# A local attention feeding a channel-mix block on one Trainium2 core: the first unit of tokens multiplied in fp32 on weights that are not yet split

## The chip, the cores and the metric

The kernel runs on one core of a Trainium2 chip. TensorE (PE in the profile, with PEld for its weight loads) multiplies into PSUM; VectorE (DVE), ScalarE (ACT) and GpSimd (POOL) work on tiles of 128 partitions; SyncE (SP) issues every DMA. The metric is device time in microseconds of one launch. Three runs of the kernel before gave 420.61, 421.57 and 421.47 us, a median of 421.47 us.

## The reference

Two stages follow one another. The first is attention over short windows: q, k and v are 4 batches x 8 heads x 768 tokens x 64. Tokens stand in chunks of 32, and each chunk sees 8 memory keys, its own 32 keys, 16 to the left and 8 to the right. The second stage is a channel mix over the 512 features that the heads give together:

```python
scores = scale * np.matmul(q_c, k_full.transpose(0, 1, 3, 2))   # per chunk of 32 queries, 64 keys
a = np.exp(scores - max); a = a / (np.sum(a) + 1e-09); out = np.matmul(a, v_full)
...
xk = mu_k * x + (1.0 - mu_k) * x_prev        # x_prev: the token before
xr = mu_r * x + (1.0 - mu_r) * x_prev
k = np.maximum(xk @ w_k, 0.0)                # w_k 512 x 1024
v = k * k @ w_v                              # w_v 1024 x 512
r = 1.0 / (1.0 + np.exp(-(xr @ w_r)))        # w_r 512 x 512
return r * v
```

Here x has 3072 rows (4 x 768) of 512 features. All of it is fp32.

## The kernel before, in words

**Units.** The 3072 tokens are cut into 12 units of 256 tokens (`UTOK`); a unit is two tiles of 128. For each unit the kernel makes scores (PE `s`), a softmax (DVE `mx`, `e`, `sum`; ACT exp on `e`), a transposition of the probabilities (PE `pt`), copies into a block layout (`aTz`), the product with v (PE `px`), a copy to the transposed features `xT`, and then the channel mix: the gate `g` (PE `pr`, two blocks, sigmoid `sg`), the key side `h` (PE `ph`, four blocks, relu and square `kf`) and the value side `v` (PE `pv`, four half blocks), a product with the gate (`o`) and a store.

**Split products.** A product of fp32 accuracy is made of three passes in a reduced format, fp32r: an operand is split into a high part (a cast) and a low part (operand minus high part), and TensorE adds high x high, high x low and low x high. So every weight tile, every `xf` and every `kf` gets a cast and a subtraction (`wkh`/`wkl`, `wvh`/`wvl`, `wrh`/`wrl`, `xh`/`xl`, `kh`/`kl`) ahead of its first product. One block of `g`, `h` or `v` is 12 matmuls of 512 columns or 24 of 256.

**Weights.** The weights come as 64-bit words, ten DMAs of 1 MB into `raw`: two of w_r, four of w_k, four of w_v, in this order. Each needs an ACT pass (`mag`, L270), a DVE shift (L273), a DVE join to fp32 (L277), then the cast and the subtraction (L283).

**Order.** The order on every engine is written ahead of time by a planner in the file. `te_order` gives each PE operation a due time from a list: `LEAD` for the start and one pattern per unit. `Plan.order` then lists operations greedily with an assumed cost for each, and picks an engine where an operation has alternatives; buffer tags with fixed counts (`bufs`) add waits. Where the plan leaves PE idle before the first `ph`, products of zeros or of a weight tile (`warm`, L660 and L663) are put in; L660 holds three lists written out by hand for the three longest gaps.

**Around the change.** `weight` prepares one weight tile, `scores` a unit's softmax, `prep` the two mixes `xf` and their split, `channel_mix` the blocks of `g`, `h` and `v`. The first unit is handled as every other is.

Of the kernel before, what the change touches and what calls it, by code (L numbers as in the profile page):

```python
# [29 lines left out]
LOOK = 400  # L30
EASE = 0.0
LEAD = "s0 t0 t1 a0 a1 s1 g0.0 g0.1"
# [7 lines left out]
BLOCK = 2.65  # L40
PE_COST = {"s": 1.6, "t": 0.4, "a": 1.05, "g": BLOCK, "h": BLOCK, "v": BLOCK}
# [33 lines left out]
class Plan:  # L75
# [40 lines left out]
    def order(self):  # L116
        self.dues()
# [3 lines left out]
        for q in todo.values():  # L121
            q.sort(key=lambda o: (o.due, o.seq))
        done = []
        while len(done) < len(self.ops):
            best = None
            for q in todo.values():
# [20 lines left out]
def te_order():  # L147

    nu = B * S // UTOK
    seq = LEAD.split()  # L150
    seq = [tuple([x[0]] + [int(n) for n in x[1:].split(".")]) for x in seq]
    for u in range(nu):
# [17 lines left out]
def local_attention__then__channel_mix(  # L170
# [31 lines left out]
    def split_tiles(n, name):  # L202
        return [
            [const.tile([P, 2 * DM], F32R, tag=f"{name}{s}{i}", name=f"{name}{s}{i}") for i in range(n)]
            for s in "hl"
        ]

    wk_hl, wv_hl, wr_hl = split_tiles(KT, "wk"), split_tiles(FT // 2, "wv"), split_tiles(KT // 2, "wr")
# [6 lines left out]
    zero_r = const.tile([P, 2 * DM], F32R, tag="zeror", name="zero_r")  # L215
    nc.vector.memset(zero_sb, 0.0)
    nc.vector.memset(zero_r.bitcast(F32), 0.0)
# [24 lines left out]
    wdone = {}  # L242
# [4 lines left out]
    def weight(i):  # L247
        src, (hi, lo), k = chunks[i]
        h, l = hi[k], lo[k]
# [18 lines left out]
        def f_abs():  # L268
            m = T["mag", i] = sb("x4", [P, 2 * DM], f"mag{i}")
# [5 lines left out]
        def f_join():  # L275
            mi = T["mag", i].bitcast(U32)
            nc.vector.scalar_tensor_tensor(mi, mi, 3, word(0, U32), ALU.logical_shift_left, ALU.bitwise_or)  # L277

        def f_hi(e):
            copy(e, h, T["mag", i])  # L280

        def f_lo(e):
            e.tensor_sub(l, T["mag", i], h.bitcast(F32))  # L283

        raw, mag = Slot("big"), Slot("x4")
        a = op(("dma", 3.0), f_load, new=[raw])
# [4 lines left out]
        ll = op(either(dve=(1.15, True), pool=(2.5, True)), f_lo, [hh], use=[mag])  # L291
        wdone[id(hi), k] = (hh, ll)

    def wdeps(hl, ks):
        return [o for k in ks for o in wdone[id(hl[0]), k]]

    xdone = {}
    prior = {}
# [3 lines left out]
    def scores(u):  # L302


        ts = range(u * QPU, (u + 1) * QPU)

# [5 lines left out]
        def f_s():  # L312
            s = T["s", u] = ps("s", f"s{u}", QPU)
            s5 = s.rearrange("p (h c r k) -> p h c r k", h=2, c=QPU, r=NPAIR)
            nq = NPAIR * NJ * CHUNK
            for c, t in enumerate(ts):
                a = T["qk", t]
                q4 = a[:, :nq].rearrange("p (r j q) -> p r j q", r=NPAIR, j=NJ)
                k4 = a[:, nq:].rearrange("p (r j k) -> p r j k", r=NPAIR, j=NJ)
                for r in range(NPAIR):  # L320
                    for j in range(NJ):
                        for h in range(2):
                            z = slice(64 * h, 64 * h + 64)
                            nc.tensor.matmul(  # L324
                                s5[CHUNK * j : CHUNK * (j + 1), h, c, r, :], q4[z, r, j, :], k4[z, r, j, :],
                                start=True, stop=True,
                            )

        def f_max():
            s5 = T["s", u].rearrange("p (h c r k) -> p h c r k", h=2, c=QPU, r=NPAIR)  # L330
            for c, t in enumerate(ts):
                if qts[t][1] == 0:
                    nc.vector.memset(s5[0:CHUNK, :, c, :, 0:LEFT], NEG)
                if qts[t][1] == NQT - 1:
                    nc.vector.memset(s5[P - CHUNK : P, :, c, :, LEFT + CHUNK : LEFT + CHUNK + RIGHT], NEG)
            mx = T["mx", u] = sb("sm", [P, NG], f"mx{u}")
            nc.vector.reduce_max(mx, T["s", u].rearrange("p (g k) -> p g k", k=NK), axis=AX.X)

        def f_sub():
            e = T["e", u] = sb("e", [P, NG, NK], f"e{u}")  # L340
            nc.vector.tensor_sub(  # L341
                e,
                T["s", u].rearrange("p (g k) -> p g k", k=NK),
                T["mx", u].unsqueeze(2).to_broadcast([P, NG, NK]),
            )

        def f_exp():
            e = T["e", u]
            nc.scalar.activation(e, e, AF.Exp, scale=SCALE)  # L349

        def f_sum():
            sm = T["sum", u] = sb("sm", [P, NG], f"sum{u}")
            nc.vector.reduce_sum(sm, T["e", u], axis=AX.X)
            nc.vector.tensor_scalar_add(sm, sm, 1e-9)
            nc.vector.reciprocal(sm, sm)

        def f_norm(g):
            e = T["e", u]
            g.tensor_mul(e, e, T["sum", u].unsqueeze(2).to_broadcast([P, NG, NK]))

        qs = [Slot("big") for _ in ts]
        s1, m1, m2, e = Slot("s"), Slot("sm"), Slot("sm"), Slot("e")
        ds = due["s", u]
        l = [op(("dma", 2.3), lambda t=t: f_load(t), new=[x]) for t, x in zip(ts, qs)]
        o_s = op(("pe", 1.6), f_s, l + [prior.get("s")], new=[s1], use=qs, due=ds)
        o_m = op(("dve", 1.15), f_max, [o_s], new=[m1], use=[s1], due=ds + 4)
        o_b = op(("dve", 1.15), f_sub, [o_m], new=[e], use=[s1, m1], due=ds + 5.5)
        o_e = op(("act", 1.0), f_exp, [o_b], use=[e])
        o_u = op(("dve", 1.55), f_sum, [o_e], new=[m2], use=[e])
        o_n = op(either(dve=(1.15, True), pool=(2.2, True)), f_norm, [o_u], use=[e, m2])  # L370
        prior.update(s=o_s)
        return o_n, e

    def attention(t, o_n, e):
# [54 lines left out]
        lv = op(("dma", 1.5), f_loadv, new=[vs])  # L429
# [13 lines left out]

    def prep(u):
# [9 lines left out]
        for m in (1, 0):  # L454
            def f_mix(m=m):
                d = T["df", u]
                f = T["xf", u, m] = sb("x4", [P, KT, UTOK], f"xf{u}") if m else d
# [19 lines left out]
            fs, hs, ls = Slot("x4") if m else ds, Slot(f"xh{m}"), Slot(f"xl{m}")  # L477
# [239 lines left out]
```

## Time and profile before

The profiled execution took 420.69 us by its own time and has a span of 418.7 us; the 2.0 us between them lie outside the span.

| what | value |
|---|---|
| median of three runs | 421.47 us (420.61 to 421.57) |
| profiled execution, its own time / span | 420.69 / 418.7 us |
| PE busy, PEld busy | 409.4 us (98%), 375.4 us (90%) |
| DVE busy, ACT busy, POOL busy | 261.7 us (63%), 202.9 us (48%), 15.8 us (4%) |
| DMA moved | 48.95 MB, mean 117 GB/s |
| mean granted TensorE clock | 0.988 |

A busy PE counts the `warm` products too, so 98% says little of the start. The stages have to be read apart: the first 85.67 us, in which the first unit is worked off and the weights are prepared, and what follows, which repeats one pattern per unit. In a row of the timeline or of the chain the first number is the start in us from the span's start, the second the duration; in a row of windows, each engine's busy time with the count of its instructions, then the granted clock (PEclk), the busy share of the DMA engines and GB/s.

### The profile page before, as it was taken

Reading aid. Unit: us, or ns where it says so; the run is one execution under the profiler, and the core shown is the slowest. Engines: PE = TensorE matmul, PEld = TensorE weight load, DVE = VectorE, ACT = ScalarE, POOL = GpSimd, SP = SyncE. Lnnn points to the kernel's source line nnn. Section 1 sums busy time; section 2 is a strip of 40 time slices with the busy share of each in tenths; the row PEclk is TensorE's granted clock in tenths of the full one; section 3 lists DMA queues with packets and bytes.
Section 4 is the critical chain, followed back from the end, with each engine's and each line's share of the span. In section 5 each row is a group of like instructions: output and inputs, shape, how many; then the busy total and the mean of one; then the engine's idle time right before and its main releaser. Section 6 shows DMA issues by size and latency. Waiting matters only on the chain.

```text
span 418.7 us, 10166 instructions
## 1 busy us (share of the span) xinstructions
PE 409.4 (98%) x4601; PEld 375.4 (90%) x4601; DVE 261.7 (63%) x351; ACT 202.9 (48%) x281; POOL 15.8 (4%) x22
## 2 busy tenths in 40 slices
PE   8979999999999999999999999999999999999996
PEld 8878898799899899899898898898898898998995
DVE  2888589948729639639639539539539449447121
ACT  1642878345545445455355355364364364363150
POOL 2000001001001001001001001001001001000000
PEclk9995999999999999999999999999999999999999
DMA  8996186413313314314205206205112012100101
GB/s 315 378 363 254 66 298 216 184 52 113 140 52 126 127 50 141 124 42 163 117 25 177 101 27 193 86 29 207 68 36 95 25 57 73 38 13 2 50 2 50
DMA packets 12906, 48.95 MB, mean 117 GB/s; under 512 B 1472, under 2 KB 1600, under 8 KB 12352
## 3 DMA queue, kind: packets, MB, share of 16 engines
q1 hardware_dynamic: 12864, 48.31, 31.6%
q8 instruction: 36, 0.59, 0.6%
q14 instruction: 6, 0.05, 0.0%
HBM read 42.01 MB, written 6.29 MB: 115 GB/s over the span
## 4 chain that ended last, share of the span: by engine, by line
PE 89%; DVE 5%; ACT 3%; DMA 1%; issue 1%; ACTq 0%; SPq 0%
PE pv L588 29%; PE ph L531 29%; PE pr L492 15%; PE px L403 5%; PE s L324 4%; PE warm L660 3%; PE pt L386 2%; PE warm L663 2%; DMA raw<-in_w_v_dram 1%; ACT mag L270 1%; DVE mag L277 1%; DVE raw L273 1%; DVE wvl L283 1%; ACT e L349 1%; ACT wkh L228 0%
## 5 line engine op out<-in xcount | busy, mean ns | idle before, releaser
L531 PE MATMUL ph<-xh,wkh 128*128 128x256 f32 x384 | 107.6, 280 | 0.0
L531 PE MATMUL ph<-xl,wkh 128*128 128x256 f32 x384 | 105.6, 275 | 0.0
L531 PE MATMUL ph<-xh,wkl 128*128 128x256 f32 x384 | 105.6, 275 | 0.0
L540 ACT ACTIVATE kf<-ph 128x512 f32<-128x512 f32 x48 | 28.7, 598 | 113.9 <-PE ph L531 110.2
L531 PEld LDWEIGHTS ph<-xh,wkh 128*128 128x128 f32 x384 | 73.6, 192 | 1.1
L531 PEld LDWEIGHTS ph<-xl,wkh 128*128 128x128 f32 x384 | 73.7, 192 | 0.3
L588 PE MATMUL pv<-wvh,kh 128*128 128x512 f32 x192 | 73.8, 385 | 0.0
L531 PEld LDWEIGHTS ph<-xh,wkl 128*128 128x128 f32 x384 | 73.7, 192 | 0.0
L588 PE MATMUL pv<-wvh,kl 128*128 128x512 f32 x192 | 72.8, 379 | 0.0
L588 PE MATMUL pv<-wvl,kh 128*128 128x512 f32 x192 | 72.8, 379 | 0.0
L557 DVE TENSOR_TENSOR kl<-kf,kh 128x512 fp32r<-128x512 f32 x38 | 26.3, 691 | 55.8 <-ACT kh L228 55.6
L602 DVE TENSOR_TENSOR o<-pv,sg 128x512 f32<-128x512 f32 x24 | 16.6, 690 | 45.1 <-PE pv L588 45.1
L588 PEld LDWEIGHTS pv<-wvh,kh 128*128 128x128 f32 x192 | 36.3, 189 | 5.5
L588 PEld LDWEIGHTS pv<-wvh,kl 128*128 128x128 f32 x192 | 36.3, 189 | 5.1
L588 PEld LDWEIGHTS pv<-wvl,kh 128*128 128x128 f32 x192 | 36.3, 189 | 4.6
L492 PE MATMUL pr<-wrh,xl 128*128 128x512 f32 x96 | 37.3, 388 | 1.0 <-DVE xl L475 1.0
L492 PE MATMUL pr<-wrh,xh 128*128 128x512 f32 x96 | 37.5, 391 | 0.0
L492 PE MATMUL pr<-wrl,xh 128*128 128x512 f32 x96 | 37.3, 388 | 0.0
L547 ACT ACTIVATE kf<-kf 128x512 f32<-128x512 f32 x48 | 30.3, 631 | 1.2
L228 ACT CAST kh<-kf 128x512 fp32r<-128x512 f32 x48 | 29.8, 622 | 1.5
L349 ACT ACTIVATE e<-e 128x1024 f32<-128x1024 f32 x12 | 12.7, 1057 | 34.7 <-DVE e L341 34.7
L459 DVE SCALAR_TENSOR_TENSOR df<-df,mu_sb,xT 128x256 f32<-128x256 f32 x48 | 29.2, 667 | 0.0
(63 smaller groups left out, 547.8 us busy)
## 6 DMA issues: line engine op xcount, KB each, us to landing
qk<-in_qk_dram SPq DMA_DIRECT2D x24, 768.0 KB, 5.8
vw<-in_vw_dram SPq DMA_DIRECT2D x24, 512.0 KB, 4.5
out_dram<-o SPq DMA_DIRECT2D x24, 256.0 KB, 2.0
raw<-in_w_k_dram SPq DMA_DIRECT2D x4, 1024.0 KB, 6.7
raw<-in_w_v_dram SPq DMA_DIRECT2D x4, 1024.0 KB, 6.8
raw<-in_w_r_dram SPq DMA_DIRECT2D x2, 1024.0 KB, 10.4
id_sb<-in_ident_dram SPq DMA_DIRECT2D x1, 64.0 KB, 6.4
mu_sb<-in_mu_dram SPq DMA_DIRECT2D x1, 4.0 KB, 11.6
```

The lines of the kernel that those rows point to most:

```text
L228: e.copy(dst, src)
L324: nc.tensor.matmul(s5[CHUNK * j : CHUNK * (j + 1), h, c, r, :], q4[z, r, j, :], k4[z, r, j, :], start=True, stop=True,)
L349: nc.scalar.activation(e, e, AF.Exp, scale=SCALE)
L403: nc.tensor.matmul(p3[64 * h : 64 * h + 64, 2 * g : 2 * g + 2, CHUNK * j : CHUNK * j + CHUNK], v[:, g, h, j, :], a[:, h, g, j, :], start=True,
L459: nc.vector.scalar_tensor_tensor(f[:, k], d[:, k], mu_sb[:, m, k : k + 1], T["xT", u][:, k, :UTOK], ALU.mult, ALU.add)
L492: nc.tensor.matmul(pairs(p), x[:, k, c * P : (c + 1) * P], woven(w), start=(k + n == 0), stop=(k == KT - 1 and n == 2),)
L531: nc.tensor.matmul(pairs(p[:, i * UTOK : (i + 1) * UTOK]), w[:, fc], x[:, :, k].rearrange("p t n -> p n t"), start=(k + n == 0), stop=(k = ...
L540: e.activation(r, T["ph", u, f], AF.Relu)
L547: e.activation(q, q, AF.Square)
L557: e.tensor_sub(l, T["kf", u, f], T["kh", u, f].bitcast(F32))
L588: nc.tensor.matmul(pairs(p), x[:, tc_], woven(w), start=(f + n == 0), stop=(f == FT - 1 and n == 2))
L602: nc.vector.tensor_mul(o, T["pv", u, c], T["sg", u][:, c * DM : (c + 1) * DM])
```

## The change

The first unit (u = 0) is multiplied whole: `WHOLE = "hgv"` makes its key side, gate and value side plain fp32 products of the unsplit operands with the unsplit weight tiles. For that unit `xf` and `kf` are not split. `prep_first` makes `xf` by 128x256 slices, one ACT scale and one DVE multiply-add each, with 1 - mu from a small POOL operation. The key side of the first unit runs by rows of w_k (`f_row`): one w_k tile at a time adds to all four accumulators, so that a product can begin when the first tile is joined. The first unit's softmax runs tile by tile (`part`, half the columns each), and the second tile's exp and normalization stand ahead of the first weight's ACT pass and join.

The weights are loaded in the order w_k, w_r, w_v. Joined tiles have buffers of their own (`w0` to `w9`), and the low part of tile i goes into the buffer of tile i-1. `later` ties every cast and subtraction of a weight to the end of the first row block. `LEAD` lists the whole first unit, `STRICT` keeps PE in that list for the first 60 operations placed, the hand-written `warm` lists and their zero tile are gone, and `big` has 5 buffers, `sm` 4 and `x4` 3 (before: 4, 2 and 4).

From the key side of unit 1 on, PE's 1883 rows are the same as before in shape and order.

TensorE, from the second `px` of the first unit on, before (`s1` scores of unit 1, `pr0_0` the first gate block):

```order
L403 MATMUL px1_286<-aTz1_87,vw1_105 64x2x32 x16
L663 MATMUL warm_107<-zero_sb_88 128x128
L324 MATMUL s1_310<-qk2_207 32x64 x32
L324 MATMUL s1_310<-qk3_253 32x64 x32
L660 MATMUL warm_107<-wrh0_82 128x256 x10
L660 MATMUL warm_107<-wrh0_82 128x128 x48
L492 MATMUL pr0_0_465<-wrh0_82,xh0_1_392 128x512
L492 MATMUL pr0_0_465<-wrl0_84,xh0_1_392 128x512
L492 MATMUL pr0_0_465<-wrh0_82,xl0_1_402 128x512
```

The same place in the change (`w0` is the first joined w_k tile, `xf0_0` the unsplit key input):

```order
L443 MATMUL px1_270<-aTz1_77,vw1_188 64x2x32 x16
L776 MATMUL warm_90<-zero_sb_78 128x128 x8
L354 MATMUL s1_0_306<-qk2_244 32x64 x32
L354 MATMUL s1_0_306<-qk3_259 32x64 x32
L618 MATMUL ph0_0_382<-xf0_0_291,w0_215 128x256 x2
L618 MATMUL ph0_1_385<-xf0_0_291,w0_215 128x256 x2
L618 MATMUL ph0_2_388<-xf0_0_291,w0_215 128x256 x2
L618 MATMUL ph0_3_391<-xf0_0_291,w0_215 128x256 x2
L618 MATMUL ph0_0_382<-xf0_0_291,w1_263 128x256 x2
```

The key side has moved ahead of the gate, takes its operands unsplit, and no `warm` stands behind the scores of unit 1.

SyncE's queue, the sixth to the twelfth DMA, before:

```order
L256 DMA raw0_189<-in_w_r_dram 128x2x512
L256 DMA raw1_196<-in_w_r_dram 128x2x512
L245 DMA mu_sb_65<-in_mu_dram 128x8
L310 DMA qk2_207<-in_qk_dram 128x1536
L310 DMA qk3_253<-in_qk_dram 128x1536
L254 DMA raw2_284<-in_w_k_dram 128x1024
L254 DMA raw3_376<-in_w_k_dram 128x1024
```

And now, from the fifth on:

```order
L252 DMA raw0_140<-in_w_k_dram 128x1024
L420 DMA vw1_188<-in_vw_dram 128x1024
L243 DMA mu_sb_65<-in_mu_dram 128x8
L252 DMA raw1_195<-in_w_k_dram 128x1024
L330 DMA qk2_244<-in_qk_dram 128x1536
L330 DMA qk3_259<-in_qk_dram 128x1536
L252 DMA raw2_288<-in_w_k_dram 128x1024
```

Two w_k tiles have moved ahead of the scores' operands of unit 1; w_r has moved behind w_k.

VectorE, where the weights' low parts of w_r are made in the change (they stood ahead of the first gate before); `wl3` is the low part of the last w_k tile, `wl4` and `wl5` those of w_r:

```order
L275 SCALAR_TENSOR_TENSOR w9_527<-w9_527,raw9_501 128x1024
L519 TENSOR_TENSOR df1_582<-xT1_565 128x1024
L282 TENSOR_TENSOR wl3_587<-w3_413,wk3_69 128x1024
L529 SCALAR_TENSOR_TENSOR xf1_655<-df1_582,mu_sb_65,xT1_565 128x256 x4
L365 MEMSET s2_0_590 32x2x4x8
L367 TENSOR_REDUCE mx2_0_667<-s2_0_590 128x16
L282 TENSOR_TENSOR wl4_673<-w4_422,wr0_74 128x1024
L372 TENSOR_TENSOR e2_675<-s2_0_590,mx2_0_667 128x1024
L748 TENSOR_TENSOR o0_0_686<-pv0_0_572,sg0_514 128x512
L282 TENSOR_TENSOR wl5_689<-w5_445,wr1_75 128x1024
```

The splits now stand behind the joins of all ten weights, beside the first unit's output `o0_0`.

The diff, cut to its core:

```diff
-LEAD = "s0 t0 t1 a0 a1 s1 g0.0 g0.1"
+STRICT = 60
+WHOLE = "hgv"
+LEAD = "s0.0 s0.1 t0 a0 t1 a1 s1.0 h0.0 h0.1 h0.2 h0.3 g0.0 t2 t3 g0.1 a2 a3 v0.0.0 s2.0 v0.0.1 v0.1.0 v0.1.1 g1.0 g1.1"
+FULL = 3.5
...
-            q.sort(key=lambda o: (o.due, o.seq))
+            q.sort(key=lambda o: (rank[o] if o.alts[0][0] == "pe" else o.due, o.seq))
...
-                for o in q[:LOOK]:
+                for o in q[: 1 if e == "pe" and len(done) < STRICT else LOOK]:
...
-        "big": 4, "vw": 2, "x4": 4,
-        "e": 1, "sm": 2, "xT": 2, "kf": 2, "sg": 2, "o": 3,
+        "big": 5, "vw": 2, "x4": 3,
+        "e": 1, "sm": 4, "xT": 2, "kf": 2, "sg": 2, "o": 3,
...
-    chunks = [(w_r, wr_hl, k) for k in range(KT // 2)]
-    chunks += [(w_k, wk_hl, k) for k in range(KT)]
+    chunks = [(w_k, wk_hl, k) for k in range(KT)]
+    chunks += [(w_r, wr_hl, k) for k in range(KT // 2)]
     chunks += [(w_v, wv_hl, k) for k in range(FT // 2)]
...
-            m = T["mag", i] = sb("x4", [P, 2 * DM], f"mag{i}")
+            m = T["w", id(hi), k] = sb(f"w{i}", [P, 2 * DM], f"w{i}")
             nc.scalar.activation(m, word(1, F32), AF.Prelu, scale=TINY, alpha=-(2.0**32))
...
         def f_lo(e):
-            e.tensor_sub(l, T["mag", i], h.bitcast(F32))
+            l = lo[k] = sb(f"w{i - 1}", [P, 2 * DM], f"wl{i}", F32R)
+            e.tensor_sub(l, T["w", id(hi), k], h.bitcast(F32))
...
+    def later(o):
+        for x in wdone.values():
+            for d in x:
+                d.deps.append(o)
...
+            o_s = op(("pe", 0.1 + 1.5 * w), f_s, [l[d] for d in cs] + [prev], new=[s1], use=[qs[d] for d in cs], due=ds)
...
+            if u == 0 and c == QPU - 1:
+                prior["abs"].deps.append(o_e)
+                prior["join"].deps.append(o_n)
...
+        step = 1 if u == 0 else QPU
+        for c in range(0, QPU, step):
+            o_s, o_n = part(c, step, o_s, c == 0)
...
+    def f_rest():
+        nc.gpsimd.tensor_scalar(mu_sb[:, 2:4], mu_sb[:, 0:2], -1.0, 1.0, ALU.mult, ALU.add)
...
+    def prep_first(u):
...
+                    nc.scalar.mul(T["xf", u, m][:, k], T["xT", u][:, k, 1:], mu_sb[:, m, k : k + 1])
...
+                    nc.vector.scalar_tensor_tensor(
+                        f[:, k], T["xT", u][:, k, :UTOK], mu_sb[:, 2 + m, k : k + 1], f[:, k], ALU.mult, ALU.add
+                    )
...
+            if is_whole(u, "g"):
+                for k in range(KT):
+                    w = T["w", id(wr_hl[0]), k // 2][:, k % 2 * DM : (k % 2 + 1) * DM]
+                    nc.tensor.matmul(
+                        p, T["xf", u, 1][:, k, c * P : (c + 1) * P], w, start=(k == 0), stop=(k == KT - 1)
+                    )
+                return
...
+        def f_row(k):
+            for f in range(FT // 2):
...
+                        nc.tensor.matmul(
+                            p[:, i * UTOK : (i + 1) * UTOK], T["w", id(wk_hl[0]), k][:, fc], T["xf", u, 0][:, k],
+                            start=(i + k == 0), stop=(k == KT - 1), skip_group_check=True,
+                        )
...
+            later(by_k[0])
...
+                    if is_whole(u, "v"):
+                        for f in [2 * f2 + i for f2 in fs for i in range(2)]:
+                            w = T["w", id(wv_hl[0]), f // 2][:, f % 2 * DM : (f % 2 + 1) * DM]
...
+                            nc.tensor.matmul(
+                                p, T["kf", u, f // 2][:, tc_], w, start=(f == 0), stop=(f == FT - 1)
+                            )
...
-        prep(u)
+        (prep if u else prep_first)(u)
...
-                if n > 0:
+                for _ in range(n):
                     warm = warm or ps("m", "warm")
-                if n > 25 and (gap := gap + 1) in fill:
-                    for a, b, n in fill[gap]:
...
                     nc.tensor.matmul(warm[:, :P], zero_sb, zero_sb, start=True, stop=True)
```

More of the change, by code (lines that the diff above doesn't have):

```diff
@@ L200, in local_attention__then__channel_mix, with high_tiles @@
     mu_sb = const.tile([P, 4, KT], F32, tag="mu", name="mu_sb")
[L202 to L208, printed above, removed]
+    def high_tiles(n, name):
+        return [const.tile([P, 2 * DM], F32R, tag=f"{name}{i}", name=f"{name}{i}") for i in range(n)], [None] * n
+    wk_hl, wv_hl, wr_hl = high_tiles(KT, "wk"), high_tiles(FT // 2, "wv"), high_tiles(KT // 2, "wr")
     aTz = [
@@ L290, in weight, with word_deps, is_whole @@
         hh = op(either(act=(0.95,), dve=(0.62, True)), f_hi, [j], use=[mag])
-        ll = op(either(dve=(1.15, True), pool=(2.5, True)), f_lo, [hh], use=[mag])
+        ll = op(either(dve=(1.15, True), pool=(2.5, True)), f_lo, [hh], new=[low], use=[mag])
+        whole[id(hi), k] = (j, mag)
+        if i == 0:
+            prior.update(abs=b, join=j)
         wdone[id(hi), k] = (hh, ll)
+    def later(o):
+        for x in wdone.values():
+            for d in x:
+                d.deps.append(o)
     def wdeps(hl, ks):
         return [o for k in ks for o in wdone[id(hl[0]), k]]
+    def word_deps(hl, ks):
+        return [whole[id(hl[0]), k][0] for k in ks], [whole[id(hl[0]), k][1] for k in ks]
+    def is_whole(u, part):
+        return u == 0 and part in WHOLE
     xdone = {}
-    prior = {}
     xslot = {}
@@ L310, in f_load @@
             nc.sync.dma_start(a, qk[b, i])
[L312 to L327, printed above, removed]
@@ L522, in channel_mix @@
         ks = []
+        by_k = []
+        ms = [Slot("m") for _ in range(FT // 2)]
+        def f_row(k):
+            for f in range(FT // 2):
+                if k == 0:
+                    T["ph", u, f] = ps("m", f"ph{u}_{f}")
+                p = T["ph", u, f]
+                for i in range(2):
+                    fc = slice((2 * f + i) * P, (2 * f + i + 1) * P)
+                    if is_whole(u, "h"):
+                        nc.tensor.matmul(
+                            p[:, i * UTOK : (i + 1) * UTOK], T["w", id(wk_hl[0]), k][:, fc], T["xf", u, 0][:, k],
+                            start=(i + k == 0), stop=(k == KT - 1), skip_group_check=True,
+                        )
+                        continue
+                    xh, xl, (wh, wl) = T["xh", u, 0], T["xl", u, 0], wk_hl
+                    for n, (w, x) in enumerate(((wh[k], xh), (wh[k], xl), (wl[k], xh))):
+                        nc.tensor.matmul(
+                            pairs(p[:, i * UTOK : (i + 1) * UTOK]), w[:, fc], x[:, :, k].rearrange("p t n -> p n t"),
+                            start=(i + k + n == 0), stop=(k == KT - 1 and n == 2), skip_group_check=True,
+                        )
+        if u == 0:
+            for k in range(KT):
+                wd, wd_use = wdeps(wk_hl, [k]), []
+                if is_whole(u, "h"):
+                    wd, wd_use = word_deps(wk_hl, [k])
+                by_k.append(
+                    op(
+                        ("pe", FULL if is_whole(u, "h") else BLOCK), lambda k=k: f_row(k),
+                        by_k[-1:] + ([mix[u, 0][0][k]] if is_whole(u, "h") else list(mix[u, 0][:2])) + wd,
+                        new=ms if k == 0 else [], use=list(mix[u, 0][2:]) + ms * (k > 0) + wd_use,
+                        due=due["h", u, k],
+                    )
+                )
+            later(by_k[0])
         for f in range(FT // 2):
```

246 lines of the change are left out of this document (143 added, 103 removed).

## The prediction

> **What bounds the kernel now.** I read the page first, then the windows by stage, then the chain of waits, and only then single rows of the timeline.
>
> ```profile
> span 418.7 us, 10166 instructions
> PE 409.4 (98%) x4601; PEld 375.4 (90%) x4601; DVE 261.7 (63%) x351; ACT 202.9 (48%) x281; POOL 15.8 (4%) x22
> ...
> 0.00:24.95 24.95, 20.94 (x403) 18.90 (x403) 14.00 (x17) 10.04 (x12) 2.39 (x9) 1.00 0.92 353
> 24.95:35.89 10.94, 10.94 (x64) 10.94 (x59) 10.84 (x18) 5.60 (x5) 0.00 (x0) 0.74 0.63 232
> 35.89:43.39 7.50, 7.50 (x26) 6.22 (x27) 4.51 (x4) 0.61 (x2) 0.00 (x0) 0.70 0.81 323
> 43.39:55.13 11.74, 11.26 (x94) 9.67 (x92) 8.36 (x10) 11.47 (x13) 0.00 (x0) 1.00 0.35 117
> 55.13:85.67 30.54, 29.53 (x333) 26.69 (x330) 28.92 (x36) 17.81 (x25) 1.33 (x1) 1.00 0.59 215
> 85.67:418.70 333.03, 329.18 (x3697) 303.02 (x3695) 195.09 (x269) 157.40 (x226) 12.11 (x12) 1.00 0.23 82
> ```
>
> The last row is the steady part: from unit 1's key side at 85.67 us PE works 329.18 of 333.03 us, and the rest is mostly the tail behind the last product. Whatever comes there is PE's own work. In the rows above, PE is just as busy, but with what?
>
> ```profile
> 22.01 2.24 issue
> 25.02 11.08 PE warm L660 x58
> 36.10 7.47 PE pr L492 x24
> 56.70 6.14 DMA raw<-in_w_v_dram
> 75.63 5.02 PE pr L492 x22
> 85.83 5.36 PE ph L531 x48
> 91.19 0.87 PE pt L386 x8
> 94.74 2.02 PE px L403 x64
> 102.22 1.42 PE s L324 x89
> 106.42 5.18 PE pr L492 x24
> ```
>
> From 25.02 to 36.10 us it runs `warm` products, on the chain itself: the first gate waits behind them. That gate takes 7.47 us where the later one takes 5.18, since the clock is down (0.70). A second such stretch lies in the window from 43.39 us, while ACT is busy for 11.47 of 11.74 us with weights, and the value side waits for a w_v load. So the start is bound by preparing weights; PE's useful work there could stand closer together.
>
> **What must be compared.** From unit 1's key side on, PE has the same 1883 rows in both kernels. The change therefore moves the time by as much as it moves the start of that product, now 85.67 us. The useful PE work ahead of it is also the same list, save that ten blocks are fp32.
>
> **The price of an fp32 block.**
>
> ```profile
> 1.05 5.28 PE L663 MATMUL warm<-zero_sb 128*128 128x128 f32 x23 [1.05 <-DVE zero_sb L216]
> 17.08 1.28 PE L663 MATMUL warm<-zero_sb 128*128 128x128 f32 x10
> L663 PE MATMUL warm<-zero_sb x50: 274/326/579, 1.1 to 53.3; 128*128 128x128 f32 x50
> ```
>
> One fp32 product is two matmul rows in the trace. Ten rows of 128 columns end after 1.28 us, the last one lasting about 0.274, so they start (1.28 - 0.274)/9 = 0.112 us apart; at the start, with the clock not yet up, 0.22 (5.28/23; the clock column shows 1.00 there, so the spacing tells more). Per column that is twice an fp32r pass (`ph` above: 5.36/48 = 0.112 for 256). The key side has 64 rows of 256 columns, 64 x 0.223 = 14.3 us; gate and value side 48 rows of 512, at twice 5.18/24 = 0.432, 20.7 us. Together 35.0 us, where three fp32r passes would take 26.2: the change **adds 8.8 us** of PE work. Lower bound 34.2 (passes of 256 and 512 columns at 0.112 and 0.216 leave 0.007 us that don't grow with the columns; it would be paid once per row instead of twice), upper 40 (1.28/10 a row). I take the spacing, since a block is a long run of rows.
>
> **When the first row block can start.** Rows of the first tile pair:
>
> ```profile
> qk<-in_qk_dram SPq DMA_DIRECT2D x1, 768.0 KB, 4.2
> 7.32 1.48 PE L324 MATMUL s<-qk 64*32 64x64 f32 x128
> 8.90 0.17 DVE L333 MEMSET s<- 32x128 f32 x1 [6.83 <-PE s L324]
> 9.10 1.23 DVE L337 TENSOR_REDUCE mx<-s 128x16 f32<-128x1024 f32 x1
> 10.36 1.22 DVE L341 TENSOR_TENSOR e<-s,mx 128x1024 f32<-128x1024 f32 x1
> 11.61 1.06 ACT L349 ACTIVATE e<-e 128x1024 f32<-128x1024 f32 x1 [9.59 <-DVE e L341]
> 12.70 1.22 DVE L353 TENSOR_REDUCE sum<-e 128x16 f32<-128x1024 f32 x1 [1.12 <-ACT e L349]
> 13.96 0.17 DVE L354 TENSOR_SCALAR sum<-sum 128x16 f32<-128x16 f32 x1
> 14.16 0.25 DVE L355 RECIPROCAL sum<-sum 128x16 f32<-128x16 f32 x1
> 17.06 2.36 ACT L228 COPY aTz<-pt 64x512 f32<-64x512 f32 x4
> 20.67 1.08 ACT L228 COPY xT<-px 128x512 f32<-128x512 f32 x2
> 26.20 1.66 DVE L459 SCALAR_TENSOR_TENSOR xf<-df,mu_sb,xT 128x256 f32<-128x256 f32 x4
> 0.00:22.01 22.01, 20.25 (x349) 18.29 (x349) 12.93 (x17) 8.91 (x11) 2.39 (x9) 1.00 0.91 348
> ```
>
> The first q/k tile lands at 0.74 + 4.2 = 4.9 us; ten `warm` products hold PE to 1.05 + 20 x 0.22 = 5.45, and half the scores (0.74) end at 6.2. Halves of the passes above follow: memset 0.17, max and subtraction 1.22, exp 0.53, sum 0.61 + 0.17 + 0.25, the second tile's max 0.61, normalization 0.61: 10.4, with handovers of 0.03 10.6. DVE goes on with the second tile (0.61), the first weight's shift (0.63), a copy (0.59), sum 1.03 and normalization 0.61: 14.1. Then one tile's `pt` 0.44, two copies 1.18, `px` 1.0: 16.7; `xT` 0.54, one scale and one add of 128x256 (0.42 each): the first slice stands at 18.1. The first w_k tile is there before: it has landed (3.2 MB with all ahead of it, 9.2 us at the 348 GB/s below), and its join stands right behind that normalization, 1.27 more. PE has eight `warm` products (16 x 0.112 = 1.8) to 18.5, then unit 1's scores, whose operands need 6.36 MB of loads, 18.3 us at 348 GB/s. They end at 18.5 + 1.5 = 20.0.
>
> Behind them I put the **2.24 us** of "issue" again: PE stops with 349 products done, while loads use 0.91 of the DMA engines; nothing the profile shows holds it. In the change 290 products stand ahead of the scores and 128 in them, so the 349th falls into them again. Bounds 0 and 2.24; I take the upper, since the load on the DMA is alike. First row block: **22.2 us**.
>
> **From there to unit 1's key side** PE has 35.0 us of fp32 blocks, `pt` 0.87, `px` 2.02, scores 1.42, gate of unit 1 5.18: 44.5 us, so 66.7 at the earliest. I add 1.3 for handovers (the gate waits for an accumulator that a relu of 0.60 frees, and the second softmax for DVE): **68.0 us**, 17.7 earlier. Span 418.7 - 17.7 = 401.0; profiled time 420.7 - 17.7 = 403.0; the median stands 0.8 above the profiled run: **403.8 us**.
>
> **What must hide.** Splitting all weights is moved behind the first row block, beside fp32 products.
>
> ```profile
> L277 DVE SCALAR_TENSOR_TENSOR mag<-mag,raw 128x1024 uint32<-128x1024 uint32 x10 | 12.5, 1269 | 0.0
> L273 DVE TENSOR_SCALAR raw<-raw x10: 632/693/2076, 14.3 to 66.1; 128x1024 uint32<-128x1024 uint32 x10
> L283 DVE TENSOR_TENSOR wkl<-mag,wkh 128x1024 fp32r<-128x1024 f32 x4 | 4.8, 1214 | 0.1
> 66.04 1.33 POOL L557 TENSOR_TENSOR kl<-kf,kh 128x512 fp32r<-128x512 f32 x1 [62.94 <-ACT kh L228]
> 66.13 2.08 DVE L273 TENSOR_SCALAR raw<-raw 128x1024 uint32<-128x1024 uint32 x1
> ```
>
> Up to `wl5`, which unit 1's gate needs at 68.0 - 5.2 = 62.8, DVE has from 18.1 on: 8 joins 10.2, 8 shifts 5.5, 5 low parts 6.1, 8 adds 3.3, unit 1's softmax 5.3, max and subtraction of unit 2's 2.5, relu and squares about 2.8, `df`, `xf` and `o` 3.6: 39.3 us, done by 57.4 if it never waits. That leaves 5.4 us for waits: 2.2 for late scores, and POOL, whose three passes of 128x1024 are some 2.66 us each (2 x 1.33): beside one, a DVE shift of 0.69 took 2.08.
>
> **Rivals.** (1) **TensorE's clock sags in the start**, as here, and `warm` rows and first row blocks run at half.
>
> ```profile
> 30.60:40.30 9.70, 9.70 (x36) 8.79 (x36) 9.70 (x11) 2.97 (x3) 0.00 (x0) 0.50 0.60 226
> ```
>
> It was down for 9.7 us and came up 5.3 us after PE's first product. 20 `warm` products between the first `pt` and the row block cost 40 x 0.11 = 4.4 more if cold, 5.3 to 9.7 us of half clock in the blocks 2.6 to 4.9. Taken together about 5 to 7: 409 to 411. Against it: few gaps, and fp32 `warm` rows did bring the clock up. The Trainium skill ("TensorE: Matmul & The Clock Gate", Part 1) has the clock fall after an idle window of about 3.4 us. By that rule this rival would not come, as no wait in my sum is so long; but here the clock fell with PE busy for 10.94 of 10.94 us, so I don't lean on it.
>
> (2) **DVE becomes the bound**: its waits exceed 5.4 us, and unit 1's gate or key side waits 2 to 4 us for a low part: 406 to 408. For: it is nearly full. Against: the margin.
>
> (3) **Slower**: fp32 products don't keep the clock up, and the blocks run at half clock throughout: 35.0 us more, 439. It decides once 17.7 us of these blocks' time are lost, half of the blocks. Against: rows of zeros sped up from 0.22 to 0.112 in the midst of such products.
>
> (4) **The gain is not kept**: q/k or v tiles come too late for a steady part that starts earlier. Time 420 to 421. Against: the DMA share there is 0.23.
>
> **Chances.** Forecast 0.58 (without the stall and the 1.3 us 400.3; with DVE a little late 406.5; own range 399.5 to 406.5), rival (1) 0.19, (2) 0.12, (3) 0.04, (4) 0.04, better than 399.5 0.03. The range 399.5 to 411 holds the first three but the worst of (1). A measurement here can tell 0.3%, 1.3 us, from no change: faster 0.92, same 0.03, slower 0.05.
>
> **What would show it.** Right: the first `ph` row near 22 us, fp32 rows of 256 columns 0.22 us apart at a granted clock of 1.00, unit 1's key side near 68 us, no idle PE ahead of unit 1's gate, and 333 us behind it. Wrong: a clock of 0.50 anywhere from 10 to 45 us; DVE as the releaser of unit 1's `pr` or `ph`; an "issue" gap elsewhere; a steady part longer than 333 us.

## The result, and the profile after

The changed kernel takes **405.16 us** (median of 4 runs, 403.85 to 405.68), the kernel before 421.04 us (419.53 to 421.57; the three runs given above and a fourth). The ratio is **0.9624** (95% interval 0.9588 to 0.9659): 3.8% faster. The prediction said 403.8 us, with a range of 399.5 to 411. The profiled execution of the changed kernel was the longest of the four, 405.68 us with a span of 403.9 us; 403.85 us came with a span of 402.1 us and a mean granted clock of 1.000.

The head of the page, changed kernel:

```profile
span 403.9 us, 9861 instructions
PE 395.7 (98%) x4450; PEld 352.9 (87%) x4450; DVE 256.4 (63%) x347; ACT 203.6 (50%) x284; POOL 23.5 (6%) x25
```

PE's share is 98% as before, and again it says little. The windows by stage (stretch, its length, busy time and count for PE, PEld, DVE, ACT and POOL, granted clock, DMA share, GB/s), from the first row block on, cut at its end and at unit 1's key side:

```profile
25.27:40.56 15.29, 15.29 (x68) 13.27 (x67) 14.51 (x17) 12.66 (x14) 4.04 (x1) 0.92 0.98 366
40.56:71.03 30.47, 30.47 (x274) 17.63 (x273) 29.78 (x34) 20.23 (x24) 4.80 (x2) 1.00 0.70 262
71.03:403.90 332.87, 329.01 (x3697) 302.85 (x3695) 198.68 (x271) 158.64 (x227) 12.12 (x12) 1.00 0.22 78
```

The last row answers the steady part of before: 332.87 us with 329.01 us of PE, against 333.03 and 329.18. All of the gain lies ahead of unit 1's key side, which moved from 85.67 to 71.03 us. DVE is nearly full in the first two rows (29.78 of 30.47 us in the second): the splitting of the weights has not gone away, it lies beside fp32 products now.

The chain of waits of the changed kernel (start, duration, what), from the scores of unit 1 to its key side:

```profile
20.64 0.74 PE s L354 x50
21.38 2.78 issue
24.16 1.18 PE s L354 x66
25.34 15.22 PE ph L618 x64
...
41.43 6.87 PE pr L561 x16
...
50.31 3.63 PE pv L715 x8
...
55.36 10.50 PE pv L715 x24
65.86 5.18 PE pr L569 x24
71.03 5.36 PE ph L652 x48
```

Behind the first `ph` row the chain is PE's own work without a gap. Ahead of it the "issue" stop of before is there again, 2.78 us. The granted clock of 0.92 in the first row of the windows is taken up below.

### The profile page after: what moved, and what is told of

The parts are those of the page before. It is cut to its first block, busy times and chain, and to the rows that moved or that the text cites. A ratio compares the mean times of both kernels' runs of the same rounds, so it can differ in the third digit from the quotient of the medians.

```text
span 403.9 us, 9861 instructions
## 1 busy us (share of the span) xinstructions
PE 395.7 (98%) x4450; PEld 352.9 (87%) x4450; DVE 256.4 (63%) x347; ACT 203.6 (50%) x284; POOL 23.5 (6%) x25
## 4 chain that ended last, share of the span: by engine, by line
PE 98%; issue 1%; DVE 0%
PE ph L652 30%; PE pv L726 29%; PE pr L569 14%; PE px L443 6%; PE s L354 4%; PE ph L618 4%; PE pv L715 3%; PE warm L776 3%; PE pt L426 3%; PE pr L561 2%; DVE o L748 0%; DVE zero_sb L215 0%
## 5 line engine op out<-in xcount | busy, mean ns | idle before, releaser
L652 PE MATMUL ph<-xh,wk 128*128 128x256 f32 x352 | 98.6, 280 | 0.0
L652 PE MATMUL ph<-xl,wk 128*128 128x256 f32 x352 | 96.8, 275 | 0.0
L652 PE MATMUL ph<-xh,wl 128*128 128x256 f32 x352 | 96.8, 275 | 0.0
L652 PEld LDWEIGHTS ph<-xh,wk 128*128 128x128 f32 x352 | 67.5, 192 | 1.0
L652 PEld LDWEIGHTS ph<-xl,wk 128*128 128x128 f32 x352 | 67.5, 192 | 0.3
L726 PE MATMUL pv<-wv,kh 128*128 128x512 f32 x176 | 67.7, 385 | 0.0
L652 PEld LDWEIGHTS ph<-xh,wl 128*128 128x128 f32 x352 | 67.6, 192 | 0.0
L726 PE MATMUL pv<-wv,kl 128*128 128x512 f32 x176 | 66.7, 379 | 0.0
L726 PE MATMUL pv<-wl,kh 128*128 128x512 f32 x176 | 66.7, 379 | 0.0
L569 PE MATMUL pr<-wr,xh 128*128 128x512 f32 x88 | 33.8, 384 | 0.0
```

The costliest lines, as they stand in the source:

```text
L569: nc.tensor.matmul(pairs(p), x[:, k, c * P : (c + 1) * P], woven(w), start=(k + n == 0), stop=(k == KT - 1 and n == 2),)
L652: nc.tensor.matmul(pairs(p[:, i * UTOK : (i + 1) * UTOK]), w[:, fc], x[:, :, k].rearrange("p t n -> p n t"), start=(k + n == 0), stop=(k = ...
L726: nc.tensor.matmul(pairs(p), x[:, tc_], woven(w), start=(f + n == 0), stop=(f == FT - 1 and n == 2))
```

## The experiments

Ten kernels were run, in three sessions, each session beside runs of the kernel before. Each is compared by its ratio to the kernel before of its own session.

### 1. The kernel before without its hand-written warm lists

The three hand-written lists give way to the plain fp32 products of zeros that the planner puts in elsewhere; no other line differs from the kernel before.

```diff
-    fill = {
-        1: [(zs, far(z, 512), 5)] + [(zs, apart(z, d), 5) for d in (128, 64, 32, 16, 8)],
...
-    }
+    fill = {}
```

> The kernel before, its three hand-written lists of `warm` products replaced by plain fp32 products of zeros for the planned gaps (32, 31 and 40 pairs of 128 columns); nothing else moves. Theory W (the gain of the change comes from multiplying the first unit on unsplit operands, so that useful products start while the splits are still being made): the first gate block starts at about 25.0 + 31 x 0.224 = 31.9 us instead of 36.1 and at full clock (5.2 us instead of 7.5), so the first key side at about 49 us instead of 55.1, and unit 1's key side about 6 us earlier: 414 to 416 us. Rival R (the loss before was the hand-written `warm` stretch and the half clock beside it, and any plan without them has the gain): two thirds or more of the 16 us, 410 us or less.

Measured: 413.28 us (413.10 to 413.85) against 420.21; ratio 0.9828 (0.9772 to 0.9883). The window of the first gate in this kernel, and the chain at unit 1's key side:

```profile
24.95:35.89 10.94, 10.94 (x78) 10.30 (x77) 10.94 (x16) 7.18 (x8) 0.00 (x0) 1.00 0.74 281
```

```profile
78.42 5.36 PE ph L531 x48
```

In the same stretch the kernel before had a granted clock of 0.74, with PE just as busy. So some 7 us of the 16 that the change gained are had by warming with other products (by the interval 5 to 10 us; neither expectation named this number). Two things went with the lists: the half clock beside them, and the 2.24 us stop in the scores of unit 1, which this trace doesn't have, so the 7 us are not the clock's alone. The other 9 us (7.4 by the traces) need the rest of the change: unit 1's key side starts at 78.42 us here, at 71.03 in the changed kernel.

### 2. The changed kernel with weights split first

`WHOLE` is empty, so the first unit is multiplied in three fp32r passes as every other is; the tie of the splits to the first row block goes, and the mixes are made by `prep`, key input first. Row order of the key side, load order, buffers and the softmax by tiles stay.

```diff
-WHOLE = "hgv"
+WHOLE = ""
...
-        for m in (1, 0):
+        for m in (1, 0) if u else (0, 1):
...
-            later(by_k[0])
...
-        (prep if u else prep_first)(u)
+        prep(u)
```

> The changed kernel with its new order of loads, its key side by rows of w_k, its softmax by tiles and its plain `warm` products, but with the first unit split like every other (three fp32r passes, no whole products; mixes made as for the other units). Theory W: PE has 8.8 us less work, but the first row block waits for casts and subtractions of x and of the first w_k tile (about 5 to 6 us later), the gate for w_r's and the value side for w_v's; unit 1's key side comes at about 78 to 82 us instead of 71: 412 to 416 us. Rival R: order and plain `warm` carry the gain; without the dearer fp32 passes the time is that of the change or less, 397 to 405 us.

Measured: 410.00 us (409.53 to 411.24); ratio 0.9751 (0.9702 to 0.9799). A window of its start:

```profile
50.00:60.00 10.00, 8.59 (x214) 7.25 (x213) 9.96 (x12) 7.00 (x13) 3.85 (x1) 1.00 0.81 272
```

Here PE's blocks are shorter, but PE idles (8.59 of 10 us) while DVE has 9.96. That is the trade in one view: 8.8 us more PE work are paid to let PE work while DVE splits. It is worth about 5 us (0.9751 against 0.9624), less than theory W expected (412 to 416 us). This kernel isn't a clean undo of one line, since the mixes are made in another way too; the 5 us hold for both together. From experiment 1 to this one are 3 us (0.9828 to 0.9751); what of them belongs to the load order, the row order and the softmax by tiles is not separated, and this kernel has a stop of 2.85 us that experiment 1's has not.

### 3. Softmax of the first unit in one piece

```diff
-LEAD = "s0.0 s0.1 t0 a0 t1 a1 s1.0 h0.0 ...
+LEAD = "s0.0 t0 t1 a0 a1 s1.0 h0.0 ...
...
-        step = 1 if u == 0 else QPU
+        step = QPU
```

> The changed kernel with the first unit's softmax in one piece (both tiles together, as before), the rest as in the change. By the chain of single passes the second tile's features come 1 to 1.5 us later than in two pieces, and nothing hides it: unit 1's key side near 72 us, 406 to 407 us. If the tile-wise softmax is a main part of the gain (the first unit's features in the kernel before stood at 21.8 us, in the change at 19.3), 408 us or more; if it hides behind the load of unit 1's scores, no change from 405.

Measured: 405.29 us (404.45 to 406.12); ratio 0.9634 (0.9585 to 0.9684), the same as the changed kernel. As a whole, the softmax by tiles brings nothing that can be measured. That is not its worth alone, since the stop moved with it. The trace has this second lesson, taken up below: the stop ahead of the first row block is not there, and the first `ph` row comes at 22.75 us instead of 25.27; then PE waits 2.20 us for VectorE ahead of the first gate.

### 4. A quarter as many warm products

The products of zeros have 512 columns instead of 128, and a quarter of their number is issued, for the same time.

```diff
-    zero_sb = const.tile([P, P], F32, tag="zero", name="zero_sb")
+    zero_sb = const.tile([P, 4 * P], F32, tag="zero", name="zero_sb")
...
-                for _ in range(n):
+                for _ in range(n // 4):
...
-                    nc.tensor.matmul(warm[:, :P], zero_sb, zero_sb, start=True, stop=True)
+                    nc.tensor.matmul(warm, zero_sb[:, :P], zero_sb, start=True, stop=True)
```

> The changed kernel with `warm` products of 512 instead of 128 columns and a quarter as many: about the same time of cover, 18 rows instead of 90. It asks what the stop of 2.8 us in unit 1's scores is. Theory I (TensorE stops at a count of its own instructions, at row 348 in both kernels, because the next block of instructions comes late over full DMA engines): the 348th row now lies just behind the scores, at the start of the first row block, so the scores run through in 1.5 us and a stop of 2 to 4 us stands two or so rows into the first row block; time 404 to 406.5 us. Rival D (the scores wait for their second tile's load, or for something tied to that time): the stop stays inside the scores, at the same place in them; time 404 to 406.

Measured: **402.13 us** (401.59 to 402.64); ratio 0.9559 (0.9513 to 0.9605), about 3 us below the changed kernel. Timeline of PE, then the chain:

```profile
22.93 1.24 PE L618 MATMUL ph<-xf,w 128*128 128x256 f32 x5 [1.10 <-issue]
```

```profile
66.95 5.36 PE ph L652 x48
```

The stop lies at PE's 348th matmul row again. With fewer warm rows ahead, that row now belongs to the key side: two `ph` rows run first, the stop shrinks to 1.10 us, and the clock stays at 1.00. Theory I has the place right and the size wrong (it said 2 to 4 us), so that the time lies below both expectations. Unit 1's key side starts 4.1 us earlier; this trace is of the fastest execution of its kernel, that of the changed kernel of the slowest.

### 5. Scores of unit 1 behind the first row block

```diff
-LEAD = "... a1 s1.0 h0.0 h0.1 ...
+LEAD = "... a1 h0.0 s1.0 h0.1 ...
-STRICT = 60
+STRICT = 66
...
-            later(by_k[0])
+            later(by_k[1])
```

> The changed kernel with the scores of unit 1 moved behind the first row block of the key side (all else the same; the casts and subtractions of the weights now wait for the second row block, so that VectorE's work keeps its place). Theory S (the 2.78 us stop comes because the short score rows use up PE's instructions before the next 16 KB of them, whose transfer starts at 21.8 us and lets PE go on at 24.2, have come; 3.5 us of row block ahead of the scores hide it): first ph row at 20.5 to 21.0 instead of 25.3, no issue gap over 0.6 us, no window at clock 0.50, so unit 1's key side 3 to 4 us earlier unless VectorE, which had 0.65 us to spare, holds it: 401.5 to 403.5 us. Rival M (the stop belongs to the count of rows, about 348, and not to what stands there): the same 2 to 2.8 us stop again at the 348th row, now in the scores behind the row block, and 404.5 to 406 us.

Measured: 403.94 us (402.72 to 404.11); ratio 0.9601 (0.9573 to 0.9629). PE's timeline, then the first products of unit 1's key side:

```profile
20.32 3.72 PE L618 MATMUL ph<-xf,w 128*128 128x256 f32 x16
23.98 1.49 PE L354 MATMUL s<-qk 64*32 64x64 f32 x128
```

```profile
67.90 0.38 PE L652 MATMUL ph<-xl,wk 128*128 128x256 f32 x1 [0.74 <-DVE xl L545]
```

The 348th row is a score row here too, and there is no stop: rival M, a stop that belongs to the count alone, has fallen. The first row block comes 5.0 us earlier, but the scores, which had filled a wait, now cost 1.5 us on the chain, and unit 1's key side waits 0.74 us for VectorE's low part. What is left is 3.1 us by the trace (71.03 to 67.90), which again sets this kernel's fastest execution against the other's slowest. By the ratios only 1 us is left, within their intervals, and the median lies above the 401.5 to 403.5 us of theory S.

### 6. No large subtraction on GpSimd

```diff
-        ll = op(either(dve=(1.15, True), pool=(2.5, True)), f_lo, [hh], new=[low], use=[mag])
+        ll = op(either(dve=(1.15, True), pool=(99.0, True)), f_lo, [hh], new=[low], use=[mag])
...
-            o_l = op(either(dve=(1.15, True), pool=(2.4, True)), f_lo, [o_h], new=[ls], use=[fs, hs])
+            o_l = op(either(dve=(1.15, True), pool=(99.0, True)), f_lo, [o_h], new=[ls], use=[fs, hs])
```

> The changed kernel with GpSimd kept out of the subtractions of 128x1024 (its price in the plan is 99 us, so VectorE makes all low parts of weights and of xf). Theory P (a pass on GpSimd costs VectorE about 2 us in the instruction beside it, where the pass itself costs VectorE 1.22): VectorE gains 0.8 us a pass, three passes up to unit 1's key side, 2.4 us; the time moves little since TensorE is the chain: 404 to 405.5 us, with the last low part of unit 1's x standing 2 us or more ahead of its product instead of 0.65. Rival Q (GpSimd's passes are free work beside VectorE): VectorE gets 3 x 1.22 us more, 0.65 of it hidden, so unit 1's key side waits 3 us for VectorE: 407.5 to 409 us.

Measured: 405.03 us (403.18 to 405.55); ratio 0.9628 (0.9593 to 0.9664), the same. DVE and POOL in the timeline of the changed kernel:

```profile
30.45 4.04 POOL L282 TENSOR_TENSOR wl<-w,wk 128x1024 fp32r<-128x1024 f32 x1 [17.65 <-ACT wk L226]
33.41 1.10 DVE L383 TENSOR_SCALAR sum<-sum 128x16 f32<-128x16 f32 x1
...
56.77 2.35 POOL L545 TENSOR_TENSOR xl<-xf,xh 128x1024 fp32r<-128x1024 f32 x1 [22.29 <-ACT xh L226]
56.99 3.21 DVE L282 TENSOR_TENSOR wl<-w,wr 128x1024 fp32r<-128x1024 f32 x1
...
62.99 3.75 DVE L529 SCALAR_TENSOR_TENSOR df<-df,mu_sb,xT 128x256 f32<-128x256 f32 x4
63.21 2.46 POOL L282 TENSOR_TENSOR wl<-w,wv 128x1024 fp32r<-128x1024 f32 x1 [4.09 <-DVE wl L282]
...
68.83 1.55 DVE L545 TENSOR_TENSOR xl<-df,xh 128x1024 fp32r<-128x1024 f32 x1
```

and of this one:

```profile
55.85 1.22 DVE L282 TENSOR_TENSOR wl<-w,wr 128x1024 fp32r<-128x1024 f32 x1
...
61.00 1.66 DVE L529 SCALAR_TENSOR_TENSOR df<-df,mu_sb,xT 128x256 f32<-128x256 f32 x4
...
64.20 1.48 DVE L545 TENSOR_TENSOR xl<-df,xh 128x1024 fp32r<-128x1024 f32 x1
```

Beside a POOL pass of 2.35 us a subtraction takes 3.21 us on DVE, alone 1.22; beside one of 2.46 us four adds take 3.75, alone 1.66. Such a pass handed to POOL costs DVE 2.0 to 2.1 us, where doing it costs 1.22. The first of the three passes went otherwise: POOL itself took 4.04 us, and DVE lost some 1 us, most of it in a small instruction that ends with that pass (1.10 us, 0.17 in this kernel). Theory P holds in its direction: with three passes more on DVE, the last low part is done at 65.68 us, 3.8 us ahead of its product's block at 69.52, where the changed kernel had 0.6 us to spare (70.38 against 70.98). The time doesn't move, since PE is the chain. The Trainium skill ("SBUF — State Buffer", Terms) says that VectorE and GpSimd share a port pair and that the one without it is blocked for the other's full instruction. The trace agrees: the subtraction lost 2.0 us to a pass that went on for 2.13 us after its start.

### 7. No warm products at all

```diff
-                for _ in range(n):
+                for _ in range(0 * n):
```

> The changed kernel without any product of zeros (62 fewer fp32 products ahead of the first row block). Theory C (the clock of the first row blocks hangs on how much work TensorE did ahead of them, which is what the rival of a sagging clock was priced by): with 1.4 us scores, transpositions and px alone the blocks start at half clock, and 5 to 10 us of them cost 2.6 to 4.9 us: first ph at 20 to 21.5, unit 1's key side at 70 to 72, 403 to 406 us, that is no gain against the changed kernel although its 2.78 us stop is gone or elsewhere. Rival N (the zeros do nothing for the clock): clock 1.00 in the blocks, unit 1's key side near 67, 401 to 402.5 us.

Measured: 404.36 us (402.14 to 405.83); ratio 0.9615 (0.9567 to 0.9662). Timeline, chain and windows of its start:

```profile
19.83 2.06 PE L354 MATMUL s<-qk 64*32 64x64 f32 x128
21.82 8.52 PE L618 MATMUL ph<-xf,w 128*128 128x256 f32 x37
```

```profile
38.79 1.32 PE pt L426 x8
40.11 8.30 PE pr L561 x16
```

```profile
40.00:42.00 2.00, 2.00 (x4) 0.92 (x4) 2.00 (x3) 1.95 (x5) 0.00 (x0) 0.50 1.04 421
```

Neither theory holds as written: unit 1's key side (71.15 us) and the time lie where theory C put them, but by another cause. The key side of the first unit isn't at half clock: its first 37 rows take 8.52 us, 0.23 each, where 0.223 is the full rate, so the zeros are not needed ahead of it. The attention products before it do run slower without them: unit 1's scores take 2.06 us, where they take 1.48 in experiment 4. Later PE waits 2.62 us for the normalization of unit 1's softmax ahead of 38.79 us, and directly behind that wait the clock is 0.50: the transpositions take 1.32 us instead of 0.87 and the first gate 8.30 instead of 6.87. Its four runs had mean clocks of 0.998 and 0.999 (402.14 and 402.91 us) or 0.996 (405.81 and 405.83 us).

### 8. Three edits together

Experiments 4, 5 and 6 in one kernel, with no edit of its own.

> Three edits on the changed kernel together: a quarter as many warm products with 512 columns each, scores of unit 1 behind the first row block, no subtraction of 128x1024 on GpSimd. If the stop, the clock and VectorE are what the 3.1 us of the late first row block consist of, nothing is left ahead of TensorE: first ph at 19.5 to 20.5, unit 1's key side at 65 to 66.5, 398.5 to 400.5 us. If VectorE's total of work (it was busy 9.9 of 10 us from 20 to 70 us in the kernel with fewer warm rows, with 0.22 us to spare ahead of unit 1's key side) is the bound from there on, it ends as that kernel did: 401.5 to 403 us.

Measured: 401.92 us (401.78 to 402.17); ratio 0.9562 (0.9533 to 0.9590). First `ph` row at 19.87 us, as expected, unit 1's key side at 67.47 us, which was expected at 65 to 66.5. The chain:

```profile
37.06 0.50 ACT kf L667
37.55 0.04 issue
37.60 7.13 PE pr L561 x16
```

The first gate waits for a relu on ScalarE that ends at 37.56 us, behind that engine's passes over w_k and w_r tiles, and these behind the loads. The kernel with few warm rows alone had its first gate at 37.35 us, so the earlier start of PE is lost there. The time lies where the second theory put it, but not by its cause: VectorE's last low part is done at 63.73 us, 3.7 us ahead.

### 9 and 10. No warm product ahead of unit 1's scores, with and without GpSimd

Experiment 4's kernel without its warm products behind the second `px`, ahead of unit 1's scores; the second of the two has experiment 6's edit as well.

```diff
-                for _ in range(n // 4):
+                seen += 1
+                for _ in range(n // 4 if seen < 7 else 0):
```

> The kernel with few warm rows (a quarter as many, 512 columns each), and in addition none of them between the second px and the scores of unit 1. The scores then start at about 17.9 us and end at 19.4, while the first slice of xf is made (ready at 19.9 in the kernel with all three edits), so the first ph row comes at 19.9 instead of 21.2. Row 348 is now about the tenth of the key side, reached near 22; with the next instructions there at about 23, a stop of about 1 us remains. TensorE alone would have unit 1's key side at about 65.6. Theory D (VectorE is the bound from here on, since it finished 0.22 us ahead of that product in the kernel with few warm rows): unit 1's key side stays at 66.5 to 67, 401.6 to 402.5 us, with VectorE's low part of unit 1's x as what it waits for. Rival T (TensorE is still the bound): near 65.6, 400.3 to 401.3 us.

> The same kernel and no subtraction of 128x1024 on GpSimd, which gave VectorE 3 us of room in the run of that edit alone. Theory D: the bound falls back to TensorE and to the chain of loads and ScalarE passes of w_r ahead of the first gate (37.6 us in the kernel with all three edits), unit 1's key side at 65.5 to 66.3, 400.2 to 401.3 us, 0.8 to 1.5 us below the kernel that leaves GpSimd its passes. Rival T: no difference between the two.

Measured: **401.55 us** (401.26 to 401.64) with GpSimd's passes, ratio 0.9547 (0.9522 to 0.9572); 402.12 us (401.61 to 402.20) without, ratio 0.9558 (0.9533 to 0.9584). Timeline of the first:

```profile
20.10 0.86 PE L354 MATMUL s<-qk 64*32 64x64 f32 x64 [1.02 <-DMA qk<-in_qk_dram]
20.89 1.56 PE L618 MATMUL ph<-xf,w 128*128 128x256 f32 x6
23.48 12.68 PE L618 MATMUL ph<-xf,w 128*128 128x256 f32 x58 [1.03 <-issue]
...
66.85 0.19 PEld L652 LDWEIGHTS ph<-xl,wk 128*128 128x128 f32 x1 [0.40 <-DVE xl L545]
```

and of the second:

```profile
37.69 7.13 PE L561 MATMUL pr<-w,xf 128*128 128x512 f32 x16 [0.58 <-ACT kf L667]
```

Theory D holds for the first: unit 1's key side stays near 66.85 us, and what it waits for is VectorE's low part. I had missed that the scores then wait for their second q/k tile (1.02 us), so that the first row block comes at 20.89 instead of 19.9. For the second kernel theory D is wrong in its number: VectorE has 4 us of room (low part done at 63.60), but the gate waits for ScalarE as in experiment 8, and unit 1's key side comes at 67.56 us. The two times don't differ beyond their intervals, as rival T said, but TensorE alone, its reason, bounds neither. The first of the two has the lowest median seen, 401.55 us. It and the kernels of experiments 4, 8 and 10 lie within 0.6 us of each other, too near to rank.

## Why the prediction was right, and where it was off

**What must be compared: held.** Only the start moved. The steady part is 332.87 us (predicted 333.03), with 3697 rows of PE in both traces, and span plus what lies around it gives the time.

**The price of an fp32 block: held.** In the kernel of experiment 5, 16 key rows take 3.72 us at full clock, which is 14.3 us for 64 when the overlap of the last row is taken off, as predicted. The first gate (6.87) and the value side (3.63 and 10.50) together take 21.0 us (predicted 20.7). From the first row block to unit 1's key side the changed kernel takes 45.8 us, as the sum said (44.5 and 1.3 for handovers). That the total agrees so well is luck: the handovers were nearly nothing, and in their place stood a loss of 1 us at half clock (15.22 us for the 64 key rows) and 0.3 us in the gate and value side.

**When the first row block can start: mis-sized, 25.27 us instead of 22.2.** This is the whole error of 3.0 us in unit 1's key side (71.03 against 68.0). The rows of the changed kernel:

```profile
5.62 1.18 PE L354 MATMUL s<-qk 64*32 64x64 f32 x64
7.09 0.69 DVE L367 TENSOR_REDUCE mx<-s 128x8 f32<-128x512 f32 x1
11.55 0.66 PE L426 MATMUL pt<-id_sb,e 128*128 128x128 f32 x4
12.72 0.63 ACT L378 ACTIVATE e<-e 128x512 f32<-128x512 f32 x1
15.57 0.63 PE L426 MATMUL pt<-id_sb,e 128*128 128x128 f32 x4
```

The first scores took 1.18 us, where I took half of the 1.48 us of both tiles. That is not the price of a half: in experiments 5 and 6, whose first rows are the same, they took 0.88 and 0.93, and in experiment 7, without warm products, both tiles took 1.18 and 1.17, so here the clock was not up yet. Each half pass on VectorE took 0.69, where I took half of 1.22: the first `pt` came at 11.55 instead of 10.6 (11.24 and 11.29 in experiments 5 and 6). The second tile's exp was queued on ScalarE behind a copy and ended at 13.35, which put the second `pt` at 15.57 instead of 14.1. `px` and `warm` added 0.6, so the scores began at 20.57 instead of 18.5. Then the stop was 2.78 instead of 2.24 us, and the scores on both sides of it took 0.4 longer than thought. On VectorE, halving a pass doesn't halve its time.

**The "issue" stop: the place was right, the upper bound too low.** It came at the 349th row, in the scores, as said, but lasted 2.78 us where 0 to 2.24 were the bounds. What the place rested on was a count of rows, without a mechanism; the last section has what the runs say of one.

**What must hide: held, with less room.** VectorE's `wl` of w_r ended at 63.06 us, where 57.4 and 5.4 us of margin stood; the gate came at 65.86, so 2.8 us were left, and 0.6 for unit 1's key side. The wait for unit 1's scores took 2.58 us of that room, where 2.2 were set aside. POOL took more than the one stretched shift that the prediction pointed at: some 1 us beside its first pass and 2.0 beside the second.

**The rivals.** Rival (1), the sagging clock, came for a single window:

```profile
26.00:28.00 2.00, 2.00 (x7) 1.61 (x6) 2.00 (x3) 0.23 (x1) 0.00 (x0) 0.56 0.94 291
28.00:30.00 2.00, 2.00 (x11) 1.77 (x10) 2.00 (x3) 1.63 (x2) 0.00 (x0) 1.00 0.97 381
```

It was down from about 24.3 to 27.8 us, which cost 1 us and not the 5 to 7 of that rival, and it came directly behind the stop; the warm products ahead of it were not cold (16 rows in 2.05 us). By the prediction's own signs this one counts against it (a clock of 0.50 between 10 and 45 us), as does a first `ph` row at 25.27 us. Of the four runs two had a mean clock of 0.995 (405.38 and 405.68 us), one 0.998 and one 1.000. The price of that rival was low by its own terms too: 4.4 and 2.6 to 4.9 us add to 7.0 to 9.3, not to 5 to 7. Rival (2), VectorE as the bound, did not come, but by 0.6 us only: in experiments 5 and 9, where PE is earlier, it does. Rivals (3) and (4) did not come; the 332.87 us exclude (4). That the median is only 1.4 us off where unit 1's key side is 3.0 off is luck: the forecast put the median 0.8 us above the profiled run, and it lay 0.5 below it, that run being the longest of its four.

## What to carry to other kernels

Where an engine that prepares operands is the bound, TensorE can be given dearer products on unprepared operands to fill the time; here 8.8 us of added PE work were paid back with some 5 us net (experiment 2, where the mixes differ too). A gain at the head of the chain then ends at the next bound, so read the room of the others first: 4.4 to 5.4 us of earlier first row block (experiments 5, 8 and 9) became 3.1 to 4.2 us at unit 1's key side. In experiments 5 and 8 the 1.5 us of unit 1's scores had only moved behind the row block; the rest was held by VectorE's low part (5 and 9), ScalarE's relu (8) or a last stop of 1.03 us (9). And cost a half pass by a row of that size: 0.69 us, not half of 1.22.

## What the runs showed of the hardware that was not expected

**The stop at PE's 348th row goes with a transfer of instructions.** In seven traces (the kernel before, the changed one, experiments 2, 4, 6, 9 and 10) PE stops at row 348 or 349, for 1.03 to 2.85 us, whether that row is a score or a key product. In each a transfer of 16 KB on the instruction queue begins at 20.6 to 22.3 us, while loads keep the DMA engines full, and PE goes on 2.3 to 2.5 us after its start. The changed kernel between 21.7 and 22.9 us, by DMA queue (packets, MB, share of the engines):

```profile
q1 hardware_dynamic: 84, 0.48, 98.9%
q8 instruction: 1, 0.02, 5.7%
```

The other five traces fit: PE reaches its 348th row there only 2.7 us or more after the start of the transfer, and nothing stops. In experiments 5, 7 and 8 the transfer starts at 21.1, 22.6 and 21.0 us and the row at 24.4, 26.3 and 24.7; in experiments 1 and 3 the transfer comes earlier, at 17.1 and 18.6 us, and the row at 21.5 and 21.4. Why it is earlier there was not settled. The trace doesn't say whose instructions a transfer carries; that they are PE's is concluded from these coincidences.

**The clock fell behind three pauses, of 2.6 to 2.9 us, and stayed behind three of 2.2.** PE stops of 2.19 (experiment 6), 2.20 (experiment 3, ahead of the first gate) and 2.24 us (the kernel before) left the granted clock at 1.00 directly behind them; stops of 2.62 (experiment 7), 2.78 (the changed kernel) and 2.85 us (experiment 2) were each followed by 3.41 us at 0.50. The Trainium skill ("TensorE: Matmul & The Clock Gate", Part 1) gives windows of 3413 ns and a fall after at least one idle window. The length agrees; that a whole idle window is needed does not. Whether the pause's length decides or its place is open. In every trace the changes of the clock lie whole multiples of 3.41 us apart (the changed kernel's comes back at 27.75 us and falls again, behind the last product, 110 such lengths later). Counted in stretches of that grid, each of the three longer stops lies in one stretch and leaves PE busy for 0.59 to 0.80 of its 3.41 us; each of the three shorter ones lies across two and leaves 2.03 to 2.56 us in both. In the kernel before the clock was down for three such lengths, 10.24 us, with PE busy throughout. Such a stretch also comes in some executions of a kernel and not in others: experiment 3's four runs took 404.45 and 404.48 us at a mean clock of 1.000, 406.11 and 406.12 us at 0.996, 1.7 us apart, which is half of 3.41. The kernel is the same in all four, which speaks for the place; the two longer executions left no trace to show it.

**Without products of zeros the first row block still ran at the full rate** (experiment 7, one trace), with only attention products ahead of it, which themselves ran slower (2.06 us for scores that took 1.48). Which of them sufficed was not tried.
